# Weight groups formed in one buffer of seven blocks and stored by one transfer, a round's keys and values in one transfer, and another order at the end of the first stage

## The chip, the cores and the metric

One core of one Trainium2 chip. The time is the device time of one execution in microseconds (us), lower is better; the profiled execution is one of the same kind with its own time. Engines: PE (TensorE, matmuls; PEld its weight loads), ACT (ScalarE), DVE (VectorE), POOL (GpSimd), SP (SyncE, which here issues most transfers). SPq and ACTq are the queues of instructions that issue transfers.

## The reference, cut to what matters

```
attn  = sigmoid(q @ k.T / sqrt(64) - log(448)) @ v            # 4 batches, 12 heads, 448 x 64
x     = attn with the heads side by side                      # 4 x 448 x 768
h     = relu(x @ w_in); u, v = halves of h                    # 768 -> 2 x 512
gated = u * (w_spatial @ normalized(v) + b_spatial)
x     = gated @ w_out                                         # 512 -> 768
theta = x @ w_theta                                           # 768 -> 768
y     = x + w_tok_r @ (x * cos(theta)) + w_tok_i @ (x * sin(theta))
out   = y + relu(y @ w_ch)
```

## The kernel before, in words

Everything is computed in split precision: an operand is a high part (rounded) and a low part (the rest), and a product is three matmuls. The weights come as 64-bit floats and are turned into 32-bit ones on the chip, bit by bit.

**First stage: rounds of attention.** The loop over r (line 497) has 12 rounds of two head pairs each, three rounds per batch. PE runs the end scores of the next round (`end_scores`, line 220), the products with the values (`begin_attend` line 234, `attend` line 241), the scores of the next round (`scores`, line 212, ACT takes the sigmoid at line 198) and then some groups of the next layer (`uv`): for a batch, groups 0 to 2 and (for odd batches, for two batches together) 3 are v (lines 270 to 272, 512 columns), groups 4 to 7 are u (lines 68 to 70, 448 columns). UV_BY says how many groups are done by the end of each round; 20 of 30 fall into the rounds, ten behind them. Keys and queries are loaded three rounds ahead (`load_kq`, line 181), values two rounds ahead (`load_v`, line 187). DVE splits keys and queries (`split_pair`, lines 193 and 194) and makes the low halves of the attention's result X and of its last 64 columns, XL (lines 249 and 256), while ACT makes the high halves.

**Beside it: the weights, piece by piece.** A `Piece` is 128 rows by 384 to 512 columns of a weight. It is loaded as 64-bit words (`wraw`, line 93, four buffers), and turned in three steps: `low` on DVE (lines 102 and 104), `high` on ACT (line 109), `join` on DVE (line 114); the result is a tile `wq` (eight buffers). There are 51 pieces: 12 of w_in (these stay on the chip as wih and wil), 8 of w_out, 12 of w_th, 7 of w_tok, 12 of w_ch (these go back to DRAM as f_out, f_th, f_tok, f_ch). One call of `begin_pieces(n)` joins the pieces of the call before last, runs the lows of those loaded in the last call, loads n new ones, issues the stores that are due and makes two of the sums that are due. LOADS says how many pieces the up to three calls of a round load; in rounds 4 to 8 it is 2, 2 and 2.

Of w_out, w_th and w_ch, four pieces make a group (`Corners`): two by two corners, from which Strassen-like products need seven blocks. Three blocks are corners, stored from their `wq` tiles; four are sums, each made by DVE into one of four `ws` tiles. Each of the seven is stored by a transfer of its own (line 450). The order is kept by two lists:

```python
        load_pieces(n)
        for dst, t in puts:
            nc.sync.dma_start(dst, t)
        puts[:] = next_puts
        next_puts.clear()
        for f in late[:SUMS_NOW]:
            f()
        del late[:SUMS_NOW]
```

A sum put into next_puts by one call is moved to puts by the next call and stored by the one after that.

All engines but POOL follow the order that the program is written in (`manual_schedule`), each its own; SP is in order too, so a transfer that has to wait holds up those behind it.

**End of the stage.** Behind the rounds, ten groups are left (line 835); `beside` says what is done ahead of which: loading and splitting w_sp, the norms of batches 0 and 1 (class `Norm`, lines 590 to 638: statistics on DVE, line 604, a power on POOL, scaling on ACT, line 618, then high and low), and loads and splits of the first two blocks of w_out. Then `gate_pair(0)` multiplies u by the mixed v (eight `gated`, lines 654 to 660) for batches 0 and 1 and `project` (line 715) applies w_out; the same for batches 2 and 3; then the last layers follow, which the diff touches only where a block of a weight is read (`load_out`, `load_th`, `prep_ch`).

Of the kernel before, what the change touches and what calls it, by code (L numbers as in the profile page):

```python
# [53 lines left out]
def net(ctx: ExitStack, tc: tile.TileContext, kq, vd, vl, w_in, w_sp, bsp, w_out, w_th, w_tok, w_ch, out):  # L54
# [29 lines left out]
    class Single:  # L84


        def __init__(self, pool, src, nw=2, nq=2):
            n = src.shape[-1]
            self.pool, self.src, self.n, self.nq = pool, src, n, nq
            self.bits = src.dtype != F32  # L90
            if self.bits:
                self.raw = pool.tile([P, n], I64, tag="wraw", name="wraw", bufs=nw)
                nc.sync.dma_start(self.raw, src)

        def low(self):
            self.q = self.pool.tile([P, self.n], I32 if self.bits else F32, tag="wq", name="wq", bufs=self.nq)
            if not self.bits:
                nc.sync.dma_start(self.q, self.src)
                return
            w = self.raw.bitcast(I32).rearrange("p (n two) -> p n two", two=2)  # L100
            self.lo, self.hi = w[:, :, 0], w[:, :, 1]
            ve.tensor_scalar(out=self.q, in0=self.lo.bitcast(U32), scalar1=2.0 ** -29, scalar2=7.0,  # L102
                             op0=ALU.mult, op1=ALU.min)
            ve.scalar_tensor_tensor(out=self.q, in0=self.hi, scalar=-(2 ** 31), in1=self.q,  # L104
                                    op0=ALU.bitwise_and, op1=ALU.bitwise_or)

        def high(self):
            if self.bits:
                se.activation(self.lo.bitcast(F32), self.hi.bitcast(F32), AF.Copy, scale=2.0 ** -112)  # L109

        def join(self):
            if not self.bits:
                return self.q
            ve.scalar_tensor_tensor(out=self.q, in0=self.lo, scalar=3, in1=self.q,  # L114
                                    op0=ALU.logical_shift_left, op1=ALU.bitwise_or)
            return self.q.bitcast(F32)

    def single(pool, src, nw=2, nq=2):
        w = Single(pool, src, nw, nq)
        w.low()  # L120
        w.high()
        return w.join()

    def prep_part(pool, hi, lo, src, c, s, r=slice(0, P)):
        q = single(pool, src[:, c, s])
        acopy(hi[:, c, s], q)
        sub(lo[r, c, s], q[r], hi[r, c, s])

    def prep(pool, hi, lo, src, cols):

        n = src.shape[-1]
        n = n // 2 if n > 512 else n
        for c in range(cols):
            for o in range(0, src.shape[-1], n):
                s = slice(o, o + n)
                r = slice(0, 64 if src is w_sp and c == 3 else P)
                prep_part(pool, hi, lo, src, c, s, r)

# [33 lines left out]
    def load_kq(n):  # L172
        b, p = divmod(n, NP)
        t = {"n": n, "a": {}, "fs": n in F32_SCORES}
        r = t["r"] = at.tile([P, 2, S], F32, tag="kqr", name="kqr", bufs=4)
        if n == 0:
            nc.scalar.dma_start(r[:, 0, :P], kq[b, p, :, 0, :P])
            nc.sync.dma_start(r[:, 1, :], kq[b, p, :, 1, :])
            nc.sync.dma_start(r[:, 0, P:], kq[b, p, :, 0, P:])
        else:  # L180
            nc.sync.dma_start(r, kq[b, p])
        return t

    def load_v(t):
        b, p = divmod(t["n"], NP)
        t["v"] = at.tile([P, 6, D], F32, tag="vr", name="vr", bufs=4)
        nc.sync.dma_start(t["v"], vd[b, p])
# [71 lines left out]
    def uv(b, g, ps=None, r=None):  # L259
        if r is None:  # L260
            r = x_p.tile([P, DH], F32, tag="ev", name="ev", bufs=2)
        if ps is None:
            ps = banks("psd")[:, 0, :]
        if g < 4:
            for k in range(KC):
                if g < 3:
                    xh, xlo = (xs[b, k][:, i, g * P:(g + 1) * P] for i in range(2))
                else:
                    xh, xlo = (xl[b // 2, k][:, i].rearrange("p b t -> p (b t)") for i in range(2))
                te.matmul(ps, xh, wih[:, k, DH:], start=k == 0, stop=False)  # L270
                te.matmul(ps, xh, wil[:, k, DH:], start=False, stop=False)  # L271
                ins = te.matmul(ps, xlo, wih[:, k, DH:], start=False, stop=k == KC - 1)  # L272
            acopy(r, ps, AF.Relu)
            if g < 3:
                nc.scalar.dma_start(v_d[b][g * P:(g + 1) * P, :], r)
            else:
                nc.scalar.dma_start(v_d[b - 1][L0:S, :], r[0:64])
                nc.scalar.dma_start(v_d[b][L0:S, :], r[64:P])
        else:
            f = g - 4  # L280
            fs = slice(f * P, (f + 1) * P)
            for k in range(KC):
                X = xs[b, k]
                ins = mm3(ps[:, :S], wih[:, k, fs], wil[:, k, fs], X[:, 0, :], X[:, 1, :], k == 0, k == KC - 1)
            acopy(r[:, :S], ps[:, :S], AF.Relu)
            nc.scalar.dma_start(u_d[b][fs, :], r[:, :S])
        return ins

    class Piece:


        def __init__(self, src, k, s, dst=None):
            self.src, self.k, self.s, self.dst = src, k, s, dst

        def load(self):
            self.w = Single(at, self.src[:, self.k, self.s], NW, NQ)

        def low(self):
            self.w.low()

        def high(self):
            self.w.high()

        def join(self):
            self.q = self.w.join()
            if self.dst is not None:
                later(self.dst[:, self.k, self.s], self.q)

        def part_high(self):
            if self.dst is None:  # L310
                acopy(wih[:, self.k, self.s], self.q)

        def part_low(self):
            if self.dst is None:
                sub(wil[:, self.k, self.s], self.q, wih[:, self.k, self.s])

    pieces = [Piece(chunks(w_in), k, slice(o, o + DH)) for o in (DH, 0) for k in range(KC)]

    def spilled(src, name, n):
        dst = dram.tile(list(src.shape), F32, name=name)  # L320
        pieces.extend(Piece(src, c, slice(o, o + n), dst) for c in range(src.shape[1]) for o in range(0, src.shape[2], n))
        return dst

    late, puts, next_puts = [], [], []

    def later(dst, t):
        puts.append((dst, t))

    class Corner(Piece):


        def __init__(self, src, k, s, group, j):
# [1142 lines left out]
```

## Time and profile before

| | us |
|---|---|
| median of three runs | 630.93 (630.03 to 632.41) |
| the profiled execution | 630.04 |
| its span in the trace | 628.3 |
| PE busy | 600.2 (96%) |
| DVE busy | 443.3 (71%) |
| ACT busy | 367.5 (58%) |
| DMA | 124.57 MB, mean 198 GB/s |

The mean granted clock of TensorE over the execution is 0.981 of full speed. PE is busy through most of the span, so the time can be read as PE's work plus its idle times plus what it loses at a lower clock; the first is hardly touched by the change. The first stage with its ten last groups ends near 271 us, the two gated layers with their projections near 365 us.

### The profile page before, as it was taken

The numbers are of one execution on the slowest core, as the hardware profiler recorded it, in microseconds if no ns is written. First come the engines' busy times: TensorE is split into PE (matmuls) and PEld (weight loads), VectorE is DVE, ScalarE is ACT, GpSimd is POOL, SyncE is SP. The second block draws the span as 40 slices with busy tenths as digits, with TensorE's granted clock in tenths as the row PEclk, the third lists the DMA queues.
The fourth block names the chain that finished last, engine by engine and source line by source line (L and its number), as shares of the span: only waits on it lengthen the run. The fifth ranks groups of instructions, "written<-read, shape, count | busy, mean of one in ns | idle before, by whom it ended". The sixth has DMA issues, their size and how long they took to land.

```text
span 628.3 us, 8654 instructions
## 1 busy us (share of the span) xinstructions
PE 600.2 (96%) x3203; PEld 494.8 (79%) x3203; DVE 443.3 (71%) x697; ACT 367.5 (58%) x505; POOL 9.8 (2%) x18
## 2 busy tenths in 40 slices
PE   9999999698799999998998999999999999999997
PEld 4557666456467668897997989999999999999896
DVE  4798687453768454467877888877777766898875
ACT  6796764544356532646464488866858667562540
POOL 0000000000000010100010000000000000000000
PEclk9999999797989999999998999999999999999999
DMA  8757587674788458553397579548637416844503
GB/s 306 260 209 255 191 286 259 223 248 155 265 266 312 134 201 294 181 179 109 128 318 258 151 235 190 174 82 202 200 58 231 115 70 212 276 178 148 212 30 132
DMA packets 92190, 124.57 MB, mean 198 GB/s; under 512 B 31090, under 2 KB 75508, under 8 KB 92148
## 3 DMA queue, kind: packets, MB, share of 16 engines
q1 hardware_dynamic: 87508, 116.50, 58.6%
q10 hardware_dynamic: 4640, 7.52, 3.3%
q8 instruction: 25, 0.41, 0.3%
q14 instruction: 17, 0.14, 0.1%
HBM read 76.52 MB, written 36.47 MB: 180 GB/s over the span
## 4 chain that ended last, share of the span: by engine, by line
PE 50%; DVE 18%; DMA 16%; ACT 9%; issue 5%; SPq 1%; POOL 0%; ACTq 0%; DVEq 0%; POOLq 0%
PE pt L1084 7%; PE psa L241 4%; PE pss L212 4%; PE py L1157 4%; PE py L1159 4%; PE py L1158 4%; DMA f_out<-ws 3%; DMA f_th<-ws 3%; DVE wq L114 2%; DVE kql L59 2%; PE psd L270 2%; ACT v L618 2%; DMA out_t<-o 2%; PE psd L271 1%; PE psd L272 1%
## 5 line engine op out<-in xcount | busy, mean ns | idle before, releaser
L198 ACT ACTIVATE af<-pss,bias 128x896 f32<-128x896 f32 x72 | 67.6, 1017 | 14.2 <-PE pss L212 9.9
L241 PE MATMUL psa<-af,vr 128*64 128x448 f32 x288 | 56.8, 543 | 0.0
L1159 PE MATMUL py<-wtkh,z 128*128 128x448 f32 x144 | 52.4, 364 | 0.0
L1157 PE MATMUL py<-wtkh,z 128*128 128x448 f32 x144 | 52.1, 362 | 0.0
L1158 PE MATMUL py<-wtkl,z 128*128 128x448 f32 x144 | 52.0, 361 | 0.0
L241 PEld LDWEIGHTS psa<-af,vr 128*64 128x64 f32 x288 | 19.6, 137 | 36.3 <-issue 33.7
L212 PE MATMUL pss<-kqh 64*128 64x448 f32 x138 | 29.9, 430 | 15.2 <-ACT af L198 8.7
L109 ACT ACTIVATE wraw<-wraw 128x384 f32<-128x384 f32 (+2 forms) x51 | 29.4, 605 | 25.3 <-DVE wq L102 23.0
L65 ACT ACTIVATE ev<-psd 128x448 f32<-128x448 f32 (+1 forms) x30 | 16.9, 565 | 40.2 <-PE psd L272 20.7
L212 PEld LDWEIGHTS pss<-kqh 64*128 64x128 f32 x138 | 14.1, 201 | 28.6 <-ACT af L198 12.0
L68 PE MATMUL psd<-X,wih 128*128 128x448 f32 x96 | 35.7, 372 | 0.0
L70 PE MATMUL psd<-X,wil 128*128 128x448 f32 x96 | 35.2, 366 | 0.2 <-DVE wil L59 0.2
L69 PE MATMUL psd<-X,wih 128*128 128x448 f32 x96 | 35.1, 365 | 0.0
L114 DVE SCALAR_TENSOR_TENSOR wq<-wraw,wq 128x384 int32<-128x384 int32 (+2 forms) x51 | 28.5, 593 | 8.1 <-ACT wraw L109 8.1
L104 DVE SCALAR_TENSOR_TENSOR wq<-wraw,wq 128x384 int32<-128x384 int32 (+2 forms) x51 | 30.6, 600 | 1.8
L1078 DVE TENSOR_TENSOR R<-R,xr 128x768 f32<-128x768 f32 x24 | 21.9, 954 | 11.9 <-ACT R L1099 11.9
L59 DVE TENSOR_TENSOR X<-psa,X 128x448 fp32r<-128x448 f32 x24 | 14.6, 621 | 21.2 <-ACT X L65 21.1
L1159 PEld LDWEIGHTS py<-wtkh,z 128*128 128x128 f32 x144 | 27.0, 188 | 2.1 <-DVE z L59 0.3
L1158 PEld LDWEIGHTS py<-wtkl,z 128*128 128x128 f32 x144 | 27.0, 187 | 1.8
L270 PE MATMUL psd<-wih,X 128*128 128x512 f32 x72 | 28.4, 394 | 0.0
L1157 PEld LDWEIGHTS py<-wtkh,z 128*128 128x128 f32 x144 | 27.0, 187 | 1.4
L272 PE MATMUL psd<-wih,X 128*128 128x512 f32 x72 | 28.1, 390 | 0.0
(317 smaller groups left out, 1568.4 us busy)
## 6 DMA issues: line engine op xcount, KB each, us to landing
kqr<-in_kq SPq DMA_DIRECT2D x23, 448.0 KB, 4.7
wraw<-in_w_in SPq DMA_DIRECT2D x12, 512.0 KB, 5.7
xp<-xa SPq DMA_DIRECT2D x56, 96.0 KB, 2.5
y<-x_d SPq DMA_DIRECT2D x8, 672.0 KB, 5.2
y_d<-y SPq DMA_DIRECT2D x8, 672.0 KB, 4.2
yf<-y_d SPq DMA_DIRECT2D x8, 672.0 KB, 7.0
out_t<-o SPq DMA_DIRECT2D x23, 224.0 KB, 1.9
vr<-in_vd SPq DMA_DIRECT2D x24, 192.0 KB, 5.2
```

The lines of the kernel that those rows point to most:

```text
L68: te.matmul(ps, wh, xh, start=first, stop=False)
L69: te.matmul(ps, wh, xl, start=False, stop=False)
L70: return te.matmul(ps, wl, xh, start=False, stop=last)
L114: ve.scalar_tensor_tensor(out=self.q, in0=self.lo, scalar=3, in1=self.q, op0=ALU.logical_shift_left, op1=ALU.bitwise_or)
L198: se.activation(af, ps[:, :, :S], AF.Sigmoid, bias=bias, scale=1.0 / math.sqrt(D))
L212: te.matmul(ps[:, j, :S], t[w][a, 0, c], t[x][a, 1, :], start=n == 0, stop=n == 2)
L241: te.matmul(ps[a, :S], t["v"][:, 2 * c + j, :], t["a"][c][:, j, :], start=False, stop=c == 2)
L270: te.matmul(ps, xh, wih[:, k, DH:], start=k == 0, stop=False)
L1084: te.matmul(ps[:, :HALF], t[:, k, c], m[:, c], start=first and c == 0 and i == 0, stop=c == KH - 1 and i == 2, skip_group_check=not first)
L1157: te.matmul(o, z[:, 0, n, ds], tkh[:, c, :], start=(b, i) in heads and n == 0, stop=False)
L1158: te.matmul(o, z[:, 0, n, ds], tkl[:, c, :], start=False, stop=False)
L1159: te.matmul(o, z[:, 1, n, ds], tkh[:, c, :], start=False, stop=(b, i) in tails and n == N - 1)
```

## The change

Groups get one buffer: `Group` holds a tile `wq` of 7 x 384 columns (three buffers in place of eight small `wq` and four `ws`), a piece is turned in its slot of it, the sums are made into further slots, one of them in place of a corner that is no longer needed, and the seven blocks go out in one transfer. Pieces of w_in take groups of four too (four slots of 512), w_tok is stored four and three pieces at a time. In DRAM the seven blocks of a group stand side by side (`[P, nk, 7, HALF]` for `[P, 7, nk, HALF]`), in the order of STORED, and a block is read back through `block`. Four sums are made in one call (SUMS_NOW), and stores are issued by `flush`, which also stands at the start of a round and behind the load of the values. Keys and queries of a round are one transfer into one of two buffers, values too. Group 3 of an odd batch comes first of its batch. The last batch's v and u are collected in tiles of `wb` and stored by three transfers (besides group 3), the norms of batches 0 to 2 are spread over the last groups, w_out's first two blocks are loaded later there, and u is loaded whole.

```diff
-NQ = 8
-SUMS_NOW = 2
+NQ = 3
+SUMS_NOW = 4
+STORED = {True: ("B11", "T3", "B21", "B22", "T1", "T2", "T4"), False: ("A11", "A12", "S3", "A22", "S1", "S2", "S4")}
...
-    for tag, n, d, bufs in (("wraw", DH, I64, NW), ("wq", DH, I32, NQ), ("ws", HALF, F32, 4), ("kqr", 2 * S, F32, 4),
+    for tag, n, d, bufs in (("wraw", DH, I64, NW), ("wq", 7 * HALF, I32, NQ), ("kqr", 4 * S, F32, 2),
...
+    def load_kq(r):
+        b, p = divmod(2 * r, NP)
+        R = at.tile([P, 2, 2, S], F32, tag="kqr", name="kqr", bufs=2)
+        if r == 0:
...
+            nc.sync.dma_start(R[:, 1], kq[b, p + 1])
         else:
-            nc.sync.dma_start(r, kq[b, p])
+            nc.sync.dma_start(R, kq[b, p:p + 2].rearrange("n p i s -> p n i s"))
...
+    def load_v(ts):
+        b, p = divmod(ts[0]["n"], NP)
+        v = at.tile([P, 2, 6, D], F32, tag="vr", name="vr", bufs=2)
+        nc.sync.dma_start(v, vd[b, p:p + 2].rearrange("n p c d -> p n c d"))
...
+    class Group:
...
+        def slot(self, j):
+            if self.t is None:
+                self.t = at.tile([P, 7 * HALF], I32, tag="wq", name="wq", bufs=NQ)
+            return self.t[:, j * self.n:(j + 1) * self.n]
...
+    def cornered(src, name, by_rows):
+        nk = src.shape[1] // 2
+        dst = dram.tile([P, nk, 7, HALF], F32, name=name)
+
+        def sums(g, c):
+            q = [g.part(j) for j in range(7)]
+            x, y = (1, 2) if by_rows else (2, 1)
+
+            def first():
+                (sub if by_rows else add)(q[4], q[x], q[0] if by_rows else q[3])
...
+            def third():
+                if by_rows:
+                    sub(q[x], q[3], q[x])
+                else:
+                    sub(q[x], q[0], q[x])
+
+            def fourth():
+                sub(q[6], q[y], q[5])
+                puts.append((dst[:, c], g.whole(7)))
+
+            late.extend((first, second, third, fourth))
...
+    def block(f, by_rows, n):
+        return f[:, :, STORED[by_rows].index(n)]
...
+    def flush():
+        for dst, t in puts:
+            nc.sync.dma_start(dst, t)
+        puts.clear()
...
         load_pieces(n)
-        for dst, t in puts:
-            nc.sync.dma_start(dst, t)
-        puts[:] = next_puts
-        next_puts.clear()
+        flush()
         for f in late[:SUMS_NOW]:
...
                 ae_n = end_scores(nxt)
+            flush()
             if r + 3 < R:
-                rounds[r + 3] = [load_kq(2 * (r + 3) + i) for i in range(2)]
+                rounds[r + 3] = load_kq(r + 3)
...
             if aft:
-                for t in aft:
-                    load_v(t)
+                load_v(aft)
+            flush()
             if q == NP // 2 - 1:
-                todo += [(b, g) for g in range(8) if g != 3 or b % 2]
+                todo += [(b, g) for g in ((3, 0, 1, 2) if b % 2 else (0, 1, 2)) + (4, 5, 6, 7)]
...
         u = U[b] = pu.tile([P, FC, S], F32, tag="u", name="u", bufs=2)
+        nc.sync.dma_start(u, u_d[b].rearrange("(c p) t -> p c t", p=P))
...
-    spare = wb_p.tile([P, 3, DH], F32, tag="wb", name="ev", bufs=7)
-    norm(0)
+    held_v, held_u = (wb_p.tile([P, 3, DH], F32, tag="wb", name=n, bufs=7) for n in ("ev", "eu"))
+    held_w = wb_p.tile([P, 3, DH], F32, tag="wb", name="ew", bufs=7)
     load_bias()
     load_sp(0)
+    norm(0)
     beside = {
         0: [split_bias, lambda: load_sp(2), lambda: norm(1, pwo)],
-        1: [lambda: split_sp(0), lambda: out_load(NAMES[0], pwo, "wo"), lambda: out_load(NAMES[1], pwo, "wo")],
-        2: [lambda: N[0].stats(), lambda: split_sp(2)],
-        3: [lambda: N[0].scale()],
-        4: [lambda: N[0].high(), lambda: N[0].low()],
-        5: [lambda: N[1].stats(), lambda: out_split(NAMES[0])],
-        6: [lambda: N[1].scale()],
-        7: [lambda: N[1].high(), lambda: N[1].low()],
-        8: [lambda: out_split(NAMES[1])],
+        1: [lambda: split_sp(0), lambda: N[0].stats()],
+        2: [lambda: split_sp(2), lambda: N[1].stats()],
+        3: [lambda: N[0].scale(), lambda: N[1].bias()],
+        4: [lambda: N[0].high(), lambda: N[0].low(), lambda: norm(2)] + [lambda n=n: out_load(n, pwo, "wo") for n in NAMES[:2]],
+        5: [lambda: N[1].scaled()],
+        6: [lambda: N[1].high(), lambda: N[1].low()],
+        7: [lambda: out_split(NAMES[0]), lambda: N[2].stats()],
+        8: [lambda: out_split(NAMES[1]), lambda: N[2].bias()],
+        9: [lambda: N[2].scaled()],
     }
...
-    norm(2)
     for n in NAMES[2:4]:
         out_load(n)
     first, t = gate_pair(0, {
-        1: [lambda: N[2].stats(), lambda: out_split(NAMES[2]), lambda: out_load(NAMES[4])],
-        2: [lambda: N[2].bias()],
-        3: [lambda: N[2].scaled()],
-        4: [lambda: out_split(NAMES[3]), lambda: out_load(NAMES[5])],
-        5: [lambda: N[2].high()],
-        6: [lambda: N[2].low(), lambda: norm(3)],
+        1: [lambda: out_split(NAMES[2]), lambda: out_load(NAMES[4])],
+        2: [lambda: out_split(NAMES[3]), lambda: out_load(NAMES[5])],
+        4: [lambda: N[2].high()],
+        5: [lambda: N[2].low(), lambda: norm(3)],
     })
```

## Rows read from the trace of the kernel before

**Rows 1.** The page's 40 slices of the span, busy tenths and granted clock.
```profile
PE   9999999698799999998998999999999999999997
...
PEclk9999999797989999999998999999999999999999
```
**Rows 2.** Rounds 5 to 9: us, busy PE PEld DVE ACT POOL, PEclk, DMA share, GB/s.
```profile
84.48:102.15 17.67, 17.67 (x114) 12.14 (x113) 13.43 (x29) 10.51 (x15) 0.00 (x0) 1.00 0.87 288
102.15:132.77 30.62, 24.82 (x132) 16.57 (x131) 16.07 (x33) 13.29 (x20) 0.00 (x0) 0.89 0.75 250
132.77:161.25 28.48, 25.12 (x132) 17.48 (x131) 13.94 (x28) 11.96 (x16) 0.00 (x0) 0.88 0.56 186
161.25:186.39 25.14, 20.10 (x114) 13.21 (x113) 16.58 (x33) 12.33 (x17) 0.00 (x0) 0.86 0.81 273
186.39:209.10 22.71, 22.71 (x132) 15.50 (x131) 18.43 (x38) 12.61 (x19) 0.00 (x0) 1.00 0.77 263
```
**Rows 3.** Timeline of PE: start us, us, what, [idle before <-releaser]; round 3's groups, rounds 6 to 8.
```profile
53.74 0.50 PE L270 MATMUL psd<-wih,X 128*128 128x512 f32 x1
...
66.22 0.98 PE L220 MATMUL pse<-kqr 64*64 64x448 f32 x8
...
112.13 0.47 PE L212 MATMUL pss<-kqh 64*128 64x448 f32 x2 [2.16 <-ACT af L198]
116.64 0.74 PE L212 MATMUL pss<-kqh 64*128 64x448 f32 x2 [3.64 <-DVE X L59]
...
141.07 0.47 PE L212 MATMUL pss<-kqh 64*128 64x448 f32 x2 [0.49 <-ACT af L198]
144.82 0.74 PE L212 MATMUL pss<-kqh 64*128 64x448 f32 x2 [2.87 <-DVE X L59]
...
174.10 0.74 PE L212 MATMUL pss<-kqh 64*128 64x448 f32 x2 [5.04 <-ACT af L198]
```
**Rows 4.** Who waited for whom: us in total, times, longest us.
```profile
DVE ws L59 <- DMA f_th<-ws: 16.6, 4, 5.2
...
DVE ws L59 <- DMA f_out<-ws: 11.4, 3, 4.7
...
DVE ws L62 <- DMA f_out<-ws: 3.9, 1, 3.9
```
**Rows 5.** Timelines of SP and DVE within rounds 5 to 7.
```profile
99.55 0.96 SPq L450 DMA_DIRECT2D f_out<-ws  x2
...
104.75 0.56 DVE L62 TENSOR_TENSOR ws<-wq 128x384 f32<-128x384 f32 x1 [3.89 <-DMA f_out<-ws]
...
150.17 0.23 DVE L256 CAST XL<-X 128x128 fp32r<-128x128 f32 x1 [5.40 <-PE psd L272]
```
**Rows 6.** Busy by stretch: four microseconds across the start of round 9.
```profile
184.00:188.00 4.00, 4.00 (x29) 2.44 (x27) 3.90 (x9) 1.04 (x3) 0.00 (x0) 1.00 1.04 370
```
**Rows 7.** The start (timelines of DVE and PE, the chain of waits) and w_th's raw loads.
```profile
9.49 0.63 DVE L193 CAST kqh<-kqr 128x896 fp32r<-128x896 f32 x1 [1.25 <-DMA kqr<-in_kq]
...
11.16 0.62 DVE L193 CAST kqh<-kqr 128x896 fp32r<-128x896 f32 x1
...
30.91 0.47 PE L212 MATMUL pss<-kqh 64*128 64x448 f32 x2 [0.97 <-ACT af L198]
...
13.36 8.20 DMA wraw<-in_w_in
...
wraw<-in_w_th SPq DMA_DIRECT2D x12, 384.0 KB, 4.7
```
**Rows 8.** Timelines of PE, DVE and ACT in the two gatings.
```profile
295.33 3.85 PE L715 MATMUL pb__2866<-g,wb 128*128 128x448 f32 x18 [2.75 <-DVE u L660]
...
341.40 5.43 PE L715 MATMUL pb__3237<-g,wb 128*128 128x448 f32 x18 [2.20 <-DVE u L660]
...
278.04 0.69 DVE L604 BATCH_NORM_STATS2 st<-v 128x6 f32<-128x512 f32 x1 [1.02 <-DMA v<-v_d]
...
279.68 0.85 ACT L65 ACTIVATE wb<-wo 128x768 fp32r<-128x768 f32 x1 [6.44 <-DMA wo<-f_out]
```

More of the change, by code (lines that the diff above doesn't have):

```diff
@@ L82, in net @@
     halves = (slice(0, 64), slice(64, P))
[L84 to L137, printed above, removed]
     def chunks(w):
@@ L257, in head_ends, with uv_sums @@
         xs[b, p] = X
[L259 to L263, printed above, removed]
+    def uv_sums(b, g, ps):
         if g < 4:
@@ L298, in low @@
         def low(self):
-            self.w.low()
+            q = self.group.slot(self.j)
+            self.q = q.bitcast(F32)
+            if not self.bits:
+                nc.sync.dma_start(self.q, self.src)
+                return
+            w = self.raw.bitcast(I32).rearrange("p (n two) -> p n two", two=2)
+            self.lo, self.hi = w[:, :, 0], w[:, :, 1]
+            ve.tensor_scalar(out=q, in0=self.lo.bitcast(U32), scalar1=2.0 ** -29, scalar2=7.0,
+                             op0=ALU.mult, op1=ALU.min)
@@ L309, in part_high @@
+            self.group.came()
         def part_high(self):
-            if self.dst is None:
-                acopy(wih[:, self.k, self.s], self.q)
+            if self.hl is not None:
+                acopy(self.hl[0], self.q)
         def part_low(self):
[L314 to L321, printed above, removed]
-        return dst
@@ L324, in net @@
[L324 to L332, printed above, removed]
-            super().__init__(src, k, s)
-            self.group, self.j = group, j
-        def join(self):
-            self.q = self.w.join()
-            self.group.came(self.j, self.q)
-        def part_high(self):
-            pass
-        def part_low(self):
-            pass
-    class Corners:
-        def __init__(self, src, dst, c, by_rows, nk):
-            self.dst, self.c, self.by_rows, self.q = dst, c, by_rows, [None] * 4
+            if self.hl is not None:
+                sub(self.hl[1], self.q, self.hl[0])
@@ new lines, in net, with spilled @@
+    late, puts = [], []
+    pieces = []
+    for n in range(2 * KC):
+        if n % 4 == 0:
+            group = Group(DH, 4)
+        o, k = (DH, 0)[n // KC], n % KC
+        at_ = (slice(None), k, slice(o, o + DH))
+        pieces.append(Piece(chunks(w_in)[at_], group, n % 4, (wih[at_], wil[at_])))
+    def spilled(src, name):
+        m, n = src.shape[1:]
+        dst = dram.tile([P, m, n], F32, name=name)
+        for c in range(0, m, 4):
+            count = min(4, m - c)
+            group = Group(n, count, lambda g, c=c, count=count: puts.append((dst[:, c:c + count], g.whole(count))))
+            pieces.extend(Piece(src[:, c + j], group, j) for j in range(count))
+        return dst
@@ L473, in net @@
     with tc.manual_schedule(engines={mybir.EngineType.PE, mybir.EngineType.Activation, mybir.EngineType.DVE, mybir.EngineType.SP}):
-        rounds = {0: [load_kq(i) for i in range(2)]}
+        rounds = {0: load_kq(0)}
         se.activation(warm, mhalf, AF.Sigmoid)
@@ L491, in net @@
         ae = end_scores(rounds[0])
-        rounds[2] = [load_kq(4 + i) for i in range(2)]
+        rounds[2] = load_kq(2)
         for t in rounds[1]:
@@ L544, in net @@
             uv_now(UV_BY[r] - groups)
-        while pieces or loaded or apart or joined or late or puts or next_puts:
+        while pieces or loaded or apart or joined or late or puts:
             begin_pieces(2)
```

184 lines of the change are left out of this document (84 added, 100 removed).

## The prediction

> **What bounds the kernel now.** I read the page's slices first. In them TensorE is nearly full everywhere except in slices 8 to 11, the middle of the first stage, and it is there that its clock falls as well [rows 1]. Then I cut the stage by its rounds (one round is one pass of the loop over r; a round begins where PE runs the end scores of line 220) and asked for busy times round by round [rows 2]. Round 5 (84.48 to 102.15) and round 9 (186.39 to 209.10) are full of PE work at clock 1.00; rounds 6, 7 and 8 between them are not, and their granted clock averages 0.89, 0.88 and 0.86. The timeline of PE shows why they are long: five idle times, and after three of them the first matmul of a line that otherwise takes 0.47 us takes 0.74 [rows 3]. They end by ACT's sigmoids or DVE's X, never by a transfer, so PE only feels the second link. The first is in the list of waits: DVE's sums into `ws` wait for the stores of earlier sums, 16.6 + 11.4 + 3.9 = 31.9 us in eight waits [rows 4]. One such wait is in the timeline of DVE at 104.75, and the two stores that free its tile are issued by SP at 99.55 [rows 5], though DVE had made those sums two calls of begin_pieces earlier: a sum goes to next_puts, one call later to puts, and out in the call after that, just ahead of the sums that need its tile (four ws tiles, two sums a call). Every such call therefore waits out a whole store. Behind the sums on DVE stand the splits of keys and queries and the low halves of X, behind these the sigmoids and the banks that PE wants.
>
> **The rounds without that wait.** What PE needs for a round comes from full ones. Round 5 has two groups of line 68 (448 columns) and takes 17.67 us; round 9 has three of line 270 (512 columns) and takes 22.71 [rows 2]. One group of line 270 costs (66.22 - 53.74) / 3 = 4.16 us [rows 3]. Round 6 has the work of round 9, round 8 that of round 5, round 7 that of round 5 and one group of line 270 more, 17.67 + 4.16 = 21.83. So rounds 6 to 8 would take 62.21 us where they took 84.24: 7.91 + 6.65 + 7.47 = 22.0 us. A second way to the same sum: the five idle times are 2.16 + 3.64 + 0.49 + 2.87 + 5.04 = 14.2 us [rows 3], and the other 7.8 us are matmuls at the lower of the two clock levels (1.2 in place of 2.4 GHz), which follows idle times of 2.87 us or more here. Both go if the waits go.
>
> **Do they go?** The seven blocks now lie in one buffer, the three sums that had tiles of their own and the one made in place (T3 or S3) wait for no store, and only the first piece of the third group after waits for a buffer. By LOADS a group's four sums fall in one call and its store is issued at the next flush (round's start, after the values' load, or in the next call). Tightest is the first group of w_out: sums early in round 5, store after round 5's attend (ahead of its scores, so in the first half of the 17.67 us), buffer needed at the start of round 6, at least 8.8 us later; a store of 1.4 MB at round 5's 288 GB/s takes 4.8 us [rows 2]. It fits. The group after it is stored at round 6's start and needed late in that round, and so on by turns.
>
> DVE's work stays the same in count: four sums a group as before. The bunching moves sums into rounds that had fewer. Round 5 gets some four more at 0.56 us [rows 5], 13.43 + 2.2 = 15.7 of 17.67 us; round 8 had 16.58 with two sums that now fall into round 7, so 15.5 of 17.67. DVE is then close to PE in these two rounds, with nothing to spare for long waits. In round 7 it also waited 5.40 us for an XL tile that PE's group (1,3) still read [rows 5]; the new order runs group 3 first for odd batches, in round 6, and that wait goes, without which DVE could not keep up with a round of 21.83 us. PE's work for the reorder itself is nothing: the same groups, two of them exchanged in time.
>
> **Transfers.** The bytes stay, squeezed into less time. Rounds 6 to 8 had DMA engines busy for 0.75 x 30.62 + 0.56 x 28.48 + 0.81 x 25.14 = 59.3 us [rows 2], of 62.2 us they would be 95%; in bytes, 0.250 x 30.62 + 0.186 x 28.48 + 0.273 x 25.14 = 7.7 + 5.3 + 6.9 = 19.8 MB. Round 5 ran without PE idle at 0.87. If the engines can't be filled beyond that, the rounds need 59.3 / 0.87 = 68.2 us, 6.0 more; if they can, nothing. One 4 us stretch shows 370 GB/s beside a PE that is never idle [rows 6], and the wider rows of the stores and the spill into rounds 5 and 9 help, so I take a third, 2 us, as what remains of idle time (bounds 0 and 6, and 9 with one fall of the clock for an idle time above 2.87 us, at about 3 us each).
>
> The Trainium skill ("DMA: Bandwidth & Descriptors", Specifications) puts one core's share of HBM at about 358 GB/s. By it the 19.8 MB of these rounds would take an estimated 55 us and leave no idle time, so the sum would be 2 us lower (a part of rival (d)); the 370 GB/s of rows 6 is a little above that figure over 4 us, and no whole round here reaches it.
>
> **The start.** Keys and values of two pairs land as one. The first pair of round 1 was split at 9.49, the second right behind at 11.16 [rows 7]. With one transfer both can start only when the second has landed, at most 1.67 us later; PE wants the first only after round 0's attend and has slack, but the buffer for round 3 is released later too and the next raw load is behind it on SP. PE's 0.97 us of idle time at 30.91 [rows 7] hangs on this chain. It may grow by 1.5 or vanish: I take +0.5. From there on these loads run two rounds ahead and are hidden. SP saves 23 issues here and 53 among the stores (63 become 10), at nearly 0.5 us each [rows 5]; it spends most of its time in waits for other engines, so this is worth nothing by itself. A flush is a new place for SP to wait, for the sums of a call that DVE has begun; behind it stand the keys of three rounds ahead, or the next raw loads, which wait for later work of the same DVE anyway.
>
> **The end of the stage.** Up to the last group PE is full, so the new places of the norms there are worth nothing by themselves. In the first gating PE is idle for 2.75 us at 295.33, behind DVE's product into u [rows 8]. DVE was late since the third norm's statistics stood in its way, and these waited 1.02 us for v, while ACT waited 6.44 us for wo, both behind a store of u on SP [rows 8]. All that now runs beside the last groups, and the stores no longer use the two ev tiles. I take the 2.75 us (bounds 2.75 and 0). If the cover goes (norm 2's load waits for norm 0's low half in its only v tile), ACT waits for wo between the evictions, and PE has five banks, five groups of about 4 us, before it feels that. SP's order changes too: norm 2's loads and two loads of wo stand ahead of those of u, and wait there for norm 0; u is wanted only at the first gating, after the last groups.
>
> Against it: blocks of a weight are now read back in rows of 1.5 KB instead of one run of 3 to 4.5 KB, and u as one transfer. Where it matters is the second gating, where DVE's u is already late, 2.20 us at 341.40, and its first line then runs long (5.43 us where the same 18 matmuls took 3.85 at 295.33) [rows 8]. Half a microsecond for each, +1 (bounds 0 and +2.2, that idle time once more; no row shows such a read by itself).
>
> **Sum.** -22.0 + 2 + 0.5 - 2.75 + 1 = -21.25 us. The profiled execution took 630.04 (span 628.3), so 608.8; the median of the three runs, 630.93, is 0.89 above it, so 609.7.
>
> **Rivals.** (a) *The waits turn into waits for raw pieces.* Loads queue behind stores of 1.4 MB. A raw load behind other transfers took 8.20 us at 13.36, against a median of 4.7 for w_th [rows 7]. For: 95% of the DMA. Against: in rounds 5 and 9, at 0.87 and 0.77, PE never waited. Two or three idle times of some 3 us with a fall of the clock of about 3 each give back about 12 us in place of 2: 620.
> (b) *Slower.* The same queue, decided by one number: pieces are loaded one call before they are needed, so with a landing time L calls can't follow each other faster than about every L. Rounds 5 to 8 hold twelve calls in 17.67 + 84.24 = 101.9 us, 8.5 each. If every load took 8.5 us, nothing would be gained there; at 10 us the twelve take 120, 18 more than now, and the kernel about 648. For: the 8.20. Against: 4.7, and bytes for only 95%.
> The Trainium skill (the same page, Queues, rings and completion order) says that descriptors are consumed in ring order on each engine; the 8.20 us load agrees.
> (c) *It doesn't do what it says:* the sums no longer wait but the first piece of each group does, for a buffer, five groups in rounds 6 to 8 in place of eight waits: 5/8 of 22 us stay, 623. Against: the distances above. For: the flush can stand behind a waiting SP.
> (d) *More goes:* the 2.20 us and the slow line (1.58) of the second gating go too, and nothing stays idle in rounds 6 to 8: about 602.
>
> **How the numbers follow.** Forecast 0.70 (604 to 615), (a) 0.13, (b) 0.05, (c) 0.06, (d) 0.06. The range 602 to 620 holds the forecast, (d) and half of (a). A difference of 0.5% (3.2 us) is about what a measurement of this kernel can tell from none. All but (b) are faster; from (a) and (c) I take 0.03 for a loss of everything: faster 0.92, same 0.03, slower 0.05.
>
> **What would show it.** Rounds 6, 7 and 8 at about 23, 22 and 18 to 20 us, granted clock 1.00, no wait of DVE for a store; DMA share above 0.85 there and small waits of DVE for wraw; no idle PE in the first gating. Wrong: a wait of DVE's lows for f_out or f_th stores, long waits for wraw with a clock under 0.95, or a new idle time of PE at the start above 2 us.

## The result, and the profile after

The changed kernel takes 610.43 us (median of four runs, 608.11 to 612.08) against 631.44 for the kernel before in the runs beside it: a ratio of 0.9666, 95% interval 0.9627 to 0.9706. The forecast was 609.7 us and faster. The profiled execution took 608.11 us with a span of 606.3, 22.0 us less than the span before.

The page's slices of the kernel after, PE's busy tenths, its granted clock and DMA's share, answer to [rows 1]:

```profile
PE   8989999999999999999989999999999999999997
...
PEclk9999999999999999999998999999999999999999
...
DMA  8576578899965492833967885738638127835413
```

The hole in the middle of the first stage is gone, and so are the clock digits under 9 there; one 8 is left, at slice 22. The same rounds 5 to 9 as in [rows 2], cut at PE's end scores (us, busy PE PEld DVE ACT POOL, PEclk, DMA share, GB/s):

```profile
86.14:103.86 17.72, 17.72 (x114) 12.12 (x113) 13.76 (x30) 10.47 (x15) 0.00 (x0) 1.00 0.93 330
103.86:126.58 22.72, 22.72 (x132) 15.50 (x131) 20.37 (x42) 13.10 (x20) 0.00 (x0) 1.00 0.84 293
126.58:148.42 21.84, 21.84 (x131) 15.50 (x130) 15.46 (x30) 12.30 (x18) 0.00 (x0) 1.00 0.95 349
148.42:166.09 17.67, 17.67 (x114) 12.14 (x113) 13.33 (x26) 10.71 (x15) 0.00 (x0) 1.00 0.95 315
166.09:188.80 22.71, 22.71 (x132) 15.50 (x131) 16.38 (x34) 12.72 (x19) 0.00 (x0) 1.00 0.74 260
```

In each row PE is busy for the whole stretch at clock 1.00. Rounds 6 to 8 take 22.72 + 21.84 + 17.67 = 62.23 us; they took 84.24 [rows 2], so 22.0 us are saved there. DMA is at 0.95 in rounds 7 and 8, and no transfer holds PE up. The list of waits has no line any more in which DVE waits for a store of a group; what it waits for in its place is small (us in total, times, longest):

```profile
DVE wq L283 <- DMA wraw<-in_w_th: 2.9, 4, 1.3
...
DVE wq L283 <- DMA wraw<-in_w_tok: 1.8, 3, 1.2
```

So the rest of the change adds up to nothing. PE's timeline, for the rows that answer to the start in [rows 7] and the two gatings in [rows 8]:

```profile
32.08 0.47 PE L160 MATMUL pss<-kqh 64*128 64x448 f32 x2 [2.31 <-ACT af L146]
...
67.86 0.98 PE L168 MATMUL pse<-kqr 64*64 64x448 f32 x8
...
272.39 3.85 PE L661 MATMUL pb__2687<-g,wb 128*128 128x448 f32 x18
...
319.61 5.44 PE L661 MATMUL pb__3056<-g,wb 128*128 128x448 f32 x18 [3.35 <-DVE u L606]
```

Round 4 begins at 67.86 instead of 66.22 [rows 3]: 1.64 us lost at the start. The first gating has no idle time at its head (2.75 before), the second has 3.35 (2.20 before). Together: -22.0 + 1.64 - 2.75 + 1.15 = -21.96, the difference of the spans. The 2.31 us of idle time at 32.08 (0.97 before [rows 7]) have their cause ten microseconds earlier: DVE waits for a raw piece of w_in, which SP issued at 14.74 and which took 7.99 us to land (DVE's timeline, then the chain of waits):

```profile
22.76 0.43 DVE L283 TENSOR_SCALAR wq<-wraw 128x512 int32<-128x512 uint32 x1 [1.72 <-DMA wraw<-in_w_in]
```

```profile
14.74 7.99 DMA wraw<-in_w_in
```

Behind this piece on DVE stand the splits of keys and queries, behind these the sigmoids.

### The profile page after: what moved, and what is told of

The parts are those of the page before. It is cut to its first block, busy times and chain, and to the rows that moved or that the text cites. A ratio compares the mean times of both kernels' runs of the same rounds, so it can differ in the third digit from the quotient of the medians.

```text
span 606.3 us, 8516 instructions
## 1 busy us (share of the span) xinstructions
PE 591.5 (98%) x3203; PEld 490.4 (81%) x3203; DVE 444.8 (73%) x697; ACT 365.8 (60%) x505; POOL 10.0 (2%) x18
## 4 chain that ended last, share of the span: by engine, by line
PE 71%; DVE 11%; DMA 7%; ACT 6%; issue 3%; SPq 1%; POOLq 0%; DVEq 0%; ACTq 0%
PE pt L1048 7%; PE psa L189 6%; PE pss L160 4%; PE py L1121 4%; PE py L1123 4%; PE py L1122 4%; PE psd L214 3%; PE psd L216 3%; PE psd L69 3%; PE psd L215 3%; PE psd L71 3%; PE psd L70 3%; DMA wraw<-in_w_in 2%; PE pa__3025 L661 2%; DMA wq<-f_th 2%
## 5 line engine op out<-in xcount | busy, mean ns | idle before, releaser
L146 ACT ACTIVATE af<-pss,bias 128x896 f32<-128x896 f32 x72 | 66.2, 1021 | 5.1 <-PE pss L156 3.2
L66 ACT ACTIVATE ev<-psd 128x512 f32<-128x512 f32 (+1 forms) x26 | 14.8, 571 | 42.0 <-PE psd L71 21.9
L160 PE MATMUL pss<-kqh 64*128 64x448 f32 x138 | 27.0, 388 | 2.8 <-ACT af L146 2.8
L215 PE MATMUL psd<-wil,X 128*128 128x512 f32 x72 | 28.0, 389 | 0.0
```

Source lines behind the costliest of these rows:

```text
L146: se.activation(af, ps[:, :, :S], AF.Sigmoid, bias=bias, scale=1.0 / math.sqrt(D))
L160: te.matmul(ps[:, j, :S], t[w][a, 0, c], t[x][a, 1, :], start=n == 0, stop=n == 2)
```

## The experiments

Each experiment edits the kernel after, except for the first, which edits the kernel before; a line number belongs to the kernel that the row is from. Most experiments were timed once, in the profiled execution; the last group, with six executions of each kernel, shows how far one differs from the next.

**Eight tiles for the sums in the kernel before.** If the wait of the sums for their stores is the whole of the 22 us, more tiles alone remove it. The same number is changed in the list of tiles (`("ws", HALF, F32, 4)`).

```diff
-            return at.tile([P, HALF], F32, tag="ws", name="ws", bufs=4)
+            return at.tile([P, HALF], F32, tag="ws", name="ws", bufs=8)
...
```

> The kernel before with eight ws tiles in place of four, nothing else. Theory (DVE's wait for the stores of earlier sums is the whole loss of rounds 6 to 8): the eight waits of 31.9 us go, rounds 6 to 8 take 62 to 65 us in place of 84.2 (up to 3 may stay, since DVE still waits for the XL tiles in round 7), so 609 to 612 us. Rival (the 63 small stores on SP and in the rings hold the stage, not the tiles): rounds 6 to 8 stay above 75 us and the time above 622.

Measured: 610.11 us (607.34 to 611.56), ratio to the kernel before 0.9651, interval 0.9588 to 0.9714. Rounds 6 to 8 of this kernel, then DVE's wait for XL and PE's two gatings:

```profile
101.72:124.44 22.72, 22.72 (x132) 15.50 (x131) 19.71 (x41) 13.20 (x20) 0.00 (x0) 1.00 0.96 343
124.44:147.05 22.61, 22.54 (x131) 15.27 (x130) 12.36 (x26) 12.54 (x18) 0.00 (x0) 1.00 0.78 242
147.05:164.72 17.67, 17.67 (x114) 12.14 (x113) 13.54 (x26) 10.87 (x15) 0.00 (x0) 1.00 1.03 369
```

```profile
136.44 0.23 DVE L256 CAST XL<-X 128x128 fp32r<-128x128 f32 x1 [6.62 <-PE psd L272]
...
274.16 5.45 PE L715 MATMUL pb__2866<-g,wb 128*128 128x448 f32 x18 [3.12 <-DVE u L660]
...
321.67 5.45 PE L715 MATMUL pb__3237<-g,wb 128*128 128x448 f32 x18 [2.04 <-DVE u L660]
```

The rounds come down to 63.00 us. This kernel still makes 63 stores in place of 10, from tiles of one block each, so what counted was when a tile came free; the big buffer and the single store bring nothing more that these intervals could show. The 6.62 us wait for XL is still there and costs PE 0.77 us in round 7, not the round. Against the kernel after it keeps the fast start (round 4 at 65.73) and the idle time at the first gating (3.12 us).

**Group 3 of batch 1 late again.**

```diff
-todo += [(b, g) for g in ((3, 0, 1, 2) if b % 2 else (0, 1, 2)) + (4, 5, 6, 7)]
+todo += [(b, g) for g in ((0, 1, 2, 3) if b == 1 else (3, 0, 1, 2) if b == 3 else (0, 1, 2)) + (4, 5, 6, 7)]
```

> The kernel after with group 3 of batch 1 run last among its v groups again (batch 3 keeps the new order, since norm 2 needs it). By the prediction DVE then waits some 7 us for XL tiles in round 7 and cannot keep up: 2 to 6 us of idle PE in rounds 7 and 8, stage end later by as much. Rival (DVE has enough slack in round 8 and 9): DVE waits, PE does not, rounds 7 and 8 stay at 21.8 and 17.7 us.

Measured: 609.58 us, span 607.8. DVE's wait came back, in its timeline:

```profile
138.89 0.23 DVE L204 CAST XL<-X 128x128 fp32r<-128x128 f32 x1 [6.62 <-PE psd L216]
```

Round 7 takes 22.62 us (0.78 more), round 8 stays at 17.66. DVE stands for 6.6 us and catches up.

**Keys and queries of a round by two transfers again**, into the same two buffers.

```diff
-            nc.sync.dma_start(R, kq[b, p:p + 2].rearrange("n p i s -> p n i s"))
+            for i in range(2):
+                nc.sync.dma_start(R[:, i], kq[b, p + i])
```

> The kernel after with keys and queries of a round loaded as two transfers again, into the same two buffers. Theory (the one transfer lands later than the first half did, DVE is late, and with it the next loads): round 4 begins near 66.3 us as before, in place of 67.9. Rival (the buffers that are freed by rounds make it): it stays within 0.4 us of 67.9.

Measured: 607.50 us, span 605.7; round 4 begins at 67.50, 0.36 us earlier than after, PE idle 1.92 us at 31.00. SP's timeline in this kernel:

```profile
8.36 5.22 SPq L128 DMA_DIRECT2D kqr<-in_kq  x4
13.62 0.43 SPq L274 DMA_DIRECT2D wraw<-in_w_in  x1
```

SP still stands at the loads for round 3 until a buffer of two pairs is free, and the raw piece of w_in is queued behind them. It leaves at 13.62 here, at 14.74 in the kernel after and at 13.36 in the kernel before [rows 7]: of the 1.38 us by which the change delays it, the single transfer makes 1.12, the buffer of two pairs the rest. Little came of it, since the piece took 8.03 us to land here and DVE still waited 1.33 us for it. The 0.36 us can't be told from nothing: the eight profiles with the order of the kernel after at the start have round 4 between 66.58 and 68.73.

**The next keys and queries behind the round's first pieces** takes the piece out of that queue.

```diff
             flush()
+            begin_pieces(LOADS[r][0] if r < len(LOADS) else 1)
             if r + 3 < R:
                 rounds[r + 3] = load_kq(r + 3)
-            begin_pieces(LOADS[r][0] if r < len(LOADS) else 1)
```

> The kernel after with the load of keys and queries for three rounds ahead issued behind the first call of begin_pieces of a round, not ahead of it. Theory (at the start the raw load at 14.74 stands on SP behind a load of keys that waits for DVE to split round 1): the raw load goes out some 5 us earlier, PE's idle time of 2.31 us at 32.08 falls under 0.7, round 4 begins at 65.5 to 66.5 in place of 67.86. Rival (the bytes of the start are the bound, DMA share 0.88 in the first 20 us): round 4 begins at 67.3 or later.

Measured: 605.78 us, span 604.0. SP and PE:

```profile
9.67 0.47 SPq L273 DMA_DIRECT2D wraw<-in_w_in  x1
14.28 0.37 SPq L127 DMA_DIRECT2D kqr<-in_kq  x1
```

```profile
65.72 0.98 PE L168 MATMUL pse<-kqr 64*64 64x448 f32 x8
```

The raw piece leaves at 9.67 us in place of 14.74, DVE doesn't wait for it, and round 4 begins 2.14 us earlier. Three kernels with this order (65.72 here, 65.38 and 64.92 below) begin round 4 before all eight without it, so the gain is beyond the spread. In the profiles of all kernels PE's idle time at this place goes by DVE's wait for this piece: 0.5 to 0.7 us in the six without a wait, 0.6 us more than the wait in the other eight (waits of 0.37 to 2.07 us). The loss at the start is the raw piece's place on SP, behind a load that waits for its buffer.

**The blocks stored in the old layout**, whose read is one run of 3 to 4.5 KB and whose store has rows of 1.5 KB.

```diff
-        dst = dram.tile([P, nk, 7, HALF], F32, name=name)
+        dst = dram.tile([P, 7, nk, HALF], F32, name=name)
...
-                puts.append((dst[:, c], g.whole(7)))
+                puts.append((dst[:, :, c, :], g.whole(7)))
...
-        return f[:, :, STORED[by_rows].index(n)]
+        return f[:, STORED[by_rows].index(n)]
```

> The kernel after with the DRAM order of before for f_out, f_th and f_ch, so that a block is read back in one run of 3 to 4.5 KB and the group's store writes rows of 1.5 KB. Theory (the short rows of the read-back make ACT late in the second gating): the block's load before thh is some 0.9 us shorter, PE's idle time there falls from 3.35 to 2.2 to 2.6 us. Rival (u as one transfer makes it): the idle time stays at 3.1 to 3.5. The stage with its stores should not change (rounds 6 to 8 at 62.2, at most 1 us more).

Measured: 613.86 us, span 612.1. The DMA issues of the kernel after, then of this one (KB each, median us to landing):

```profile
f_ch<-wq SPq DMA_DIRECT2D x3, 1344.0 KB, 5.5
...
wq<-f_th SPq DMA_DIRECT2D x7, 576.0 KB, 5.0
wq<-f_ch SPq DMA_DIRECT2D x7, 576.0 KB, 5.2
...
f_out<-wq SPq DMA_DIRECT2D x2, 1344.0 KB, 5.3
```

```profile
f_ch<-wq SPq DMA_DIRECT2D x3, 1344.0 KB, 6.3
wq<-f_th SPq DMA_DIRECT2D x7, 576.0 KB, 4.5
wq<-f_ch SPq DMA_DIRECT2D x7, 576.0 KB, 4.6
f_out<-wq SPq DMA_DIRECT2D x2, 1344.0 KB, 6.4
```

The loads of 576 KB are 0.5 to 0.6 us shorter with the long run. That holds over all profiles: 4.1 to 4.6 us in the three kernels with the old layout, 4.6 to 5.3 in the eleven with the new one. The seven loads of f_out, 384 KB each, show no such difference here (5.3 us, 5.0 after). The stores are 0.8 to 1.1 us longer with short rows, but other profiles with the new layout have 5.3 to 6.1 us for f_ch and 4.9 to 6.6 for f_out, so for the stores this is not shown. The second gating's idle time was 2.08 us, inside the theory's range (the spread below takes most of the weight from it), but the first came back with 2.98 and PE waited 0.56 us in round 6. The loads behind the last stores stand later on SP here (norm 2's load of v at 240.87, at 237.73 after), which is the likely reason. As a whole the new layout is the better of the two by this one time, which is above all ten times taken of the kernel after (606.42 to 612.08 us).

**u in halves again.**

```diff
-        nc.sync.dma_start(u, u_d[b].rearrange("(c p) t -> p c t", p=P))
         for j in range(2):
             U[b, j] = u[:, j * GH:(j + 1) * GH]
+            nc.sync.dma_start(U[b, j], u_d[b][j * GH * P:(j + 1) * GH * P, :].rearrange("(c p) t -> p c t", p=P))
```

> The kernel after with u loaded in two halves again. Theory (u as one transfer makes DVE's first product of the second gating late): the wait of 1.56 us for u at 298.86 goes, and PE's idle time there falls from 3.35 to about 2.2 us, with no change in the first gating. Rival (the short rows of the blocks' read-back, as the fourth experiment's 2.08 suggests): it stays at 2.9 to 3.5.

Measured: 607.21 us, span 605.4. DVE's wait for u is gone, and PE's second gating starts with less idle time (DVE in the kernel after, then PE in this one):

```profile
298.86 0.62 DVE L606 TENSOR_TENSOR u<-psp,u 128x448 f32<-128x448 f32 x1 [1.56 <-DMA u<-u_d]
```

```profile
318.13 5.43 PE L661 MATMUL pb__3060<-g,wb 128*128 128x448 f32 x18 [1.80 <-DVE u L606]
```

1.55 us less than after. But the first gating had 1.61 us in this profile, none after, so the time tells little.

**Two buffers in place of three.**

```diff
-NQ = 3
+NQ = 2
```

> The kernel after with two buffers for groups in place of three. Theory (a buffer that is still being stored holds DVE, and DVE holds PE): the first piece of a group then meets the store of the group before last, which is issued at about that time, so DVE waits some 4 to 6 us at four or five groups in rounds 5 to 8, PE stands idle with falls of its clock, 615 to 628 us. Rival (DVE has the slack to take such waits): under 612 us.

Measured: 615.15 us, span 613.4. DVE's waits, and PE:

```profile
DVE wq L283 <- DMA f_th<-wq: 13.7, 3, 7.4
...
DVE wq L283 <- DMA f_out<-wq: 5.7, 2, 3.6
DVE wq L283 <- DMA f_tok<-wq: 4.1, 1, 4.1
```

```profile
114.48 0.47 PE L160 MATMUL pss<-kqh 64*128 64x448 f32 x2 [2.73 <-DVE X L60]
```

This is rival (c) made real: 23.5 us of DVE's waits for groups in their buffers, though PE feels only 2.73 + 0.32 us of them as idle time, and in round 6 another 1.9 us of longer matmuls (24.65 us busy where 22.72 do, at a granted clock of 0.94). Three buffers are needed, and they are enough.

**The norms at their old places**, the stores from tiles of their own and the early group 3 kept.

```diff
-        1: [lambda: split_sp(0), lambda: N[0].stats()],
-        2: [lambda: split_sp(2), lambda: N[1].stats()],
+        1: [lambda: split_sp(0), lambda: out_load(NAMES[0], pwo, "wo"), lambda: out_load(NAMES[1], pwo, "wo")],
+        2: [lambda: N[0].stats(), lambda: split_sp(2)],
...
+    norm(2)
...
```

> The kernel after with the places of before for the norms and for the loads and splits of w_out's first two blocks at the end of the first stage and in the first gating. Theory (norm 2 in the first gating makes DVE late there): PE's idle time of 2 to 3.5 us comes back in the first gating, 2 to 6 us longer with a fall of the clock. Rival (the stores from tiles of their own and the early group 3 do it): idle time under 1 us, no difference in time.

Measured: 605.48 us, span 603.7. No idle time before the first gating's head at 271.25. The norms' new places are not what took the 2.75 us away.

**The old stores of the last groups as well.** That left the stores, or the order of the groups.

```diff
-    held_v, held_u = (wb_p.tile([P, 3, DH], F32, tag="wb", name=n, bufs=7) for n in ("ev", "eu"))
-    held_w = wb_p.tile([P, 3, DH], F32, tag="wb", name="ew", bufs=7)
+    spare = wb_p.tile([P, 3, DH], F32, tag="wb", name="ev", bufs=7)
...
+        r = spare[:, k - 7, :n]
+        acopy(r, ps[:, :n], AF.Relu)
+        store_uv(b, g, r)
```

> The kernel after with both the old places of the norms and the old stores of the last groups (seven through the two ev tiles, the last three from one spare tile, one store a group); the first stage and its early group 3 stay. Theory (the stores from tiles of their own took the first gating's idle time away): the third norm's statistics wait 1 us or more for v behind the u stores, ACT waits over 4 us for wo, and PE is idle for 2.5 to 3.2 us at the head of the first gating, as in the kernel before; the time is 2.5 to 5 us above that of the experiment with the old norms alone, 608 to 611 us. Rival (the early group 3, or the fuller rounds, took it away): no idle time above 1 us there, and 605 to 607 us.

Measured: 608.92 us, span 607.1; the start of this execution is 0.87 us slower than in the first profile of the kernel after (round 4 at 68.73). The first gating has no idle time here either, so the theory falls:

```profile
273.37 3.76 PE L661 MATMUL pb__2693<-g,wb 128*128 128x448 f32 x18
```

What SP's loads of u waited for, from the list of SP's waits in the kernel before and then in this one:

```profile
SPq L646 <- DMA v_d<-ev: 8.5, 2, 4.7
```

```profile
SPq L590 <- DMA v_d<-ev: 1.2, 1, 1.2
...
SPq L542 <- DMA v_d<-ev: 6.4, 1, 6.4
```

In the kernel before these loads waited 8.5 us for stores of v out of the two ev tiles, with norm 2's v and the next w_out blocks queued behind them on SP. Here the loads of u wait less, but the store now holds norm 2's load of v (line 542) for 6.4 us, so this wait has moved more than gone. In that kernel group (3,3), with its two stores, was the sixth of the last ten groups; now it is three groups earlier. What is left of the change here is that order, norm 0's load behind the biases, u in one load and the layout. u in halves had no idle time either where the norms stood at their old places (below). The layout can't be ruled out: with the old one alone put back, and the norms at their new places, PE was idle there for 2.98 us. Neither the order of the last groups alone nor the old layout with the old norms was run, so what took the idle time away stays open.

**Together**, and the kernel after once more beside them, six executions of each. The first has the next keys and queries behind the pieces (the values stay where they were), u in halves and the old norms; the second the same with u whole.

```diff
+            begin_pieces(LOADS[r][0] if r < len(LOADS) else 1)
             if r + 3 < R:
...
+            nc.sync.dma_start(U[b, j], u_d[b][j * GH * P:(j + 1) * GH * P, :].rearrange("(c p) t -> p c t", p=P))
...
+    norm(2)
```

> The kernel after with three edits of the earlier experiments together: the next keys and values are loaded behind the first pieces of a round, u is loaded in halves, and the norms stand at their old places. Theory (the gains lie in different stretches and add): round 4 begins at 65.5 to 66.5 us, no DVE wait for u over 0.5 us, PE idle at the head of the second gating 1.8 to 2.3 us (3.35 in the kernel after), first gating under 1 us; the time is 604 to 606 us, a ratio to the kernel before of about 0.958. Rival (what the start gives is lost again at the gatings, since one look varies by about a microsecond there): 608 us or more, not told apart from the kernel after repeated beside it.

> As the combined version, but u loaded whole as in the kernel after. Theory (u's halves save their own share): DVE's wait for u of 1 to 1.6 us comes back, the second gating's idle time is about 1 us above that of the combined version, and the time is 1 us more, 605 to 607 us. Rival (u whole or in halves is worth nothing once other things are late too): the same time as the combined version within 0.5 us.

> The kernel after, unchanged, beside the two combined versions: it shows how far one profile of the same code differs from the next. If the start and the gatings vary by themselves, round 4 begins between 66.5 and 68.5 us, the head of the second gating is idle for 1.8 to 3.4 us, and the median is 607 to 611 us. If they don't, they stand at 67.9 and 3.35 us as in its first profile, and the median is 610 us.

Measured: 604.93 us for the combined version, ratio to the kernel before 0.9595 (0.9568 to 0.9621); with u whole 0.9605 (0.9579 to 0.9631); the kernel after 607.25 us, 0.9633 (0.9605 to 0.9662). PE at the second gating, in this order:

```profile
315.27 5.43 PE L661 MATMUL pb__3060<-g,wb 128*128 128x448 f32 x18 [1.94 <-DVE u L606]
```

```profile
316.44 6.50 PE L661 MATMUL pb__3056<-g,wb 128*128 128x448 f32 x18 [3.50 <-DVE u L606]
```

```profile
317.65 5.44 PE L661 MATMUL pb__3056<-g,wb 128*128 128x448 f32 x18 [2.46 <-DVE u L606]
```

The combined version is 2.3 us faster than the kernel after by the medians, with round 4 at 65.38 and no idle time at the first gating, as its theory had it. The two intervals overlap, but five of its six times (603.95 to 605.95 us, the sixth 607.43) lie below all six of the kernel after (606.42 to 611.43), so a gain of about 0.4% is likely. u in halves is worth 0.6 us by the ratios, which these intervals can't tell from nothing. With u whole the idle time rose as forecast, but not by the way that was forecast; DVE waited only 0.5 us for u:

```profile
DVE u L606 <- DMA u<-u_d: 0.5, 1, 0.5
```

Of the variation: the kernel after started round 4 at 66.75 in this profile and at 67.86 in its first, with idle times of 0.65 and 2.31 us before. In this one the raw piece left as late as 15.29 but landed in 6.32 us, and DVE did not wait for it. The second gating had 2.46 us here and 3.35 in the first; over the nine profiles with the new layout and u whole it has 1.55 to 3.50 us, the middle one 2.33, and the length of DVE's wait for u (0.5 to 1.6 us) does not order them. With u in halves it has 1.80 and 1.94, with the old layout 2.04 to 2.20 (three kernels). So at the start and at the second gating single profiles differ by up to two microseconds, and no experiment above that moved one of them by less stands on its time.

## Why the prediction was right

**What bounds it** was right. The eight waits for `ws` went, and the 22.0 us with them, by the sum that full rounds gave: 62.21 us forecast, 62.23 measured. That the wait is the cause is shown by the eight tiles in the kernel before, which alone bring 0.9651.

**Transfers** were mis-sized: of the 2 us set down for idle time that stays, nothing stayed. The DMA engines can be filled beyond round 5's 0.87, to 0.95 in two rounds here and 1.03 at 369 GB/s in round 8 of the kernel with eight tiles, with PE never idle. With that the part of rival (d) on these rounds came true; its other part, that the 2.20 us of the second gating go, did not. The Trainium skill ("DMA: Bandwidth & Descriptors", Specifications), with a limit of about 358 GB/s for a core, gave a sum without that idle time: round 7 at 349 GB/s agrees, the 369 GB/s over 17.67 us are a little above the figure, and the measurement decides. Rivals (a) and (b) fall with these rounds; the longest wait for a raw piece of w_th or w_tok was 1.3 us.

**DVE's share** was right in count and wrong in place: the moved sums fell into round 6 (20.37 us of 22.72) and not into round 5 (13.76, forecast 15.7), and round 8 had 13.33 in place of 15.5. That DVE "could not keep up" without the earlier group 3 is the step that failed outright: with it late, in the kernel with eight tiles and with group 3 of batch 1 put back, DVE waited 6.62 us for XL, and PE's round 7 was only 0.77 and 0.78 us longer.

**The start** had the right mechanism and too small a term: +0.5 forecast, +1.64 in the first profile (bound 1.5), +0.53 in the second, 0.36 to 2.51 over the eight profiles with this order. PE's 2.31 us of idle time there are also above the mark of 2 us that the prediction named as a sign of being wrong. The split of the first pair moved from 9.49 [rows 7] to 10.85 as said, and the raw load behind the buffer on SP with it, from 13.36 to 14.74. The term did not price what that load then costs: it takes 6.3 to 8.2 us to land, and DVE waits for what is left of that. With the load of keys and queries moved behind it 2.14 us come back.

**The end** came out at the forecast -2.75 for the wrong reason. Neither the norms' places nor the stores from tiles of their own are needed for it: with both put back PE is still not idle there. With the norms at their old places the first gating had no idle time in four kernels of four; with the new ones it had none in two profiles and 0.24, 0.66, 0.72, 0.90, 1.61 and 2.98 us in six. So the new places of the norms, for which I booked a gain, are rather a small loss. What made the gain stays open.

**Rows of 1.5 KB and u whole**, +1 forecast, gave +1.15 in the first profile, and that is luck: the second gave +0.26 (2.46 against 2.20), and the middle one of the nine above +0.13. Of the parts, the short rows are seen in loads 0.5 to 0.6 us longer; that u whole costs PE anything is not shown.

The errors, 2 too much in the rounds and 1.3 too little at the start and in the second gating, add to the 0.7 us by which the forecast for the profiled execution (608.8 against 608.11) missed. The large term, 22.0 us, was worked out and came true; that the small ones nearly cancel is luck.

## What to carry to other kernels

When a store frees a tile one call before the tile is needed again, ask first for more tiles: here twice as many gave all of the gain that a rebuilt buffer and a sixth of the stores gave. Add up what the limiting engine needs in the rounds that are full, and what taking a wait away can gain follows from it; here it came out to a tenth of a microsecond. When two buffers are merged into one, look at what is queued on the same issuing engine behind the load that now waits for both halves, and put what is needed sooner ahead of it.

## What was not expected of the hardware

Whether the clock falls does not go by the length of an idle time alone, and the fall can come late. In the kernel with two buffers PE was idle for 2.73 us up to 114.48. Its first matmuls afterwards took 0.47 us, the full rate, and the clock fell then, with PE at work again (stretches; the last three columns are PEclk, DMA share and GB/s):

```profile
114.40:116.00 1.60, 1.52 (x12) 1.19 (x14) 1.53 (x6) 1.60 (x3) 0.00 (x0) 0.96 1.02 410
116.00:118.00 2.00, 2.00 (x14) 1.70 (x12) 1.93 (x5) 2.00 (x3) 0.00 (x0) 0.50 0.97 276
118.00:120.00 2.00, 2.00 (x9) 1.34 (x6) 1.97 (x5) 2.00 (x4) 0.00 (x0) 0.68 0.83 315
```

0.50 is the lower of the two levels. So one slow or fast first matmul, which is how the prediction read [rows 3], does not show whether the clock held. With u in halves 1.80 us of idle time at the second gating were enough for a fall, while 1.61 us at the first gating of the same execution were not, nor 2.75 us there in the kernel before (18 matmuls in 3.85 us [rows 8]). The stretches are from the kernel with u in halves:

```profile
272.40:274.00 1.60, 1.53 (x8) 1.47 (x9) 1.05 (x1) 0.52 (x1) 0.00 (x0) 1.00 1.00 361
...
318.10:319.00 0.90, 0.86 (x3) 0.83 (x4) 0.87 (x2) 0.00 (x0) 0.00 (x0) 0.68 0.48 55
319.00:320.00 1.00, 1.00 (x4) 0.87 (x4) 0.64 (x1) 0.32 (x1) 0.00 (x0) 0.50 0.63 143
```

The start shows it at one and the same place. After 2.61 us of idle time up to 31.86 in the kernel with the old stores the clock fell from 33 us on:

```profile
33.00:34.00 1.00, 1.00 (x8) 0.92 (x6) 0.97 (x3) 1.00 (x2) 0.00 (x0) 0.52 1.08 428
```

After 2.63 us up to 32.17 in the kernel with two buffers it stayed at 1.00. The limit of 2.87 us that the prediction set for a fall does not hold below: falls followed 1.80, 2.61 and 2.73 us, and the 2.20 us at 341.40 in the kernel before, whose slow line the prediction read [rows 8] (granted clock 0.50 from 343 to 345). Of the idle times of 2.87 us and more in these profiles, each was followed by a fall. What tells the shorter cases apart stays open.
